# Mixture-of-experts kernel on one core: the first expert product contracts 128 + 64 channels instead of 96 + 96, the 64 in the two row halves of the array

## The chip, the core and the metric

The kernel runs on one core of a Trainium2 chip. Times are device microseconds (us) of a whole run of the program; lower is better. The engines of the core work side by side, each through its own list of instructions: TensorE (PE in the profile, its weight loads PEld), VectorE (DVE), ScalarE (ACT), GpSimd (POOL) and SyncE (SP, which here only issues DMAs).

## The reference

The input is 8 sequences of 3584 tokens with 192 channels, all float32. A causal convolution over 7 tokens with softmaxed weights, one set of taps for each of 8 heads of 24 channels, makes `x`. A router chooses one of 8 experts for each token, and the expert's two-layer network is applied to it:

```python
logits = np.einsum('bsd,de->bse', x, w_gate)
local_gate = 1.0 / (1.0 + np.exp(-np.einsum('bsd,de->bse', x, w_local).squeeze(-1)))
for b in range(B):
    prev_e = -1
    for s in range(S):
        fresh_e = int(np.argmax(logits[b, s]))
        e = fresh_e if s == 0 or local_gate[b, s] < 0.5 else prev_e
        prev_e = e
        p = softmax(logits[b, s])                  # sum has 1e-9 added
        h = np.maximum(x[b, s] @ w1[e], 0.0)       # w1[e]: 192 x 1024
        out[b, s] = p[e] * (h @ w2[e])             # w2[e]: 1024 x 192
```

A token with an open local gate takes the expert of the token before it.

## The kernel before

It has three stages, one after the other.

**Convolve and route** (`convolve_and_route`, lines 103 to 265). One sequence at a time, 28 tiles of 128 tokens. The convolution is a product with two banded 128 x 128 matrices a head (L165, L167), taken out of PSUM by ScalarE and VectorE alternately (L172, L170) into `y_sb`, a tile with one row of 193 values a token: 192 channels, then the gate. `y_sb` is transposed on TensorE (L177), moved to SBUF (L181, L183) and multiplied by the router's weights (L186, 9 columns). `route` works out each token's expert on VectorE, with four small transposes on TensorE (L222 to L242), writes the softmax value into the row's last column (L251) and stores the rows in DRAM as `rows` (L253, on ScalarE's DMA queue).

**Place** (`place`). Every token gets a slot; each expert's slots are filled up to whole blocks of 256. `slot_tok` holds the token of each slot, `blk_e` the expert of each block.

**Experts** (`experts`). 119 blocks of 256 slots, one after the other:

- `load` (two blocks ahead): SyncE's queue fetches the block's `w1b` (96 partitions x 2 x 1024) and `w2b`, three buffers of each; GpSimd gathers the block's 256 rows from DRAM in two indirect DMAs into `xg` (L393, four buffers).
- `hidden`: `hT = relu(w1.T x)`, 8 chunks of 128 of the 1024 hidden values. Each chunk is two matmuls of 96 contracted channels by 256 tokens (L414); two chunks share a PSUM tile `hps` of one bank, taken out in turn by ScalarE (L419) and VectorE (L417).
- `turn`: four transposes on TensorE (L402) turn the next block's `xg` into `xps`, and VectorE copies it to `xT` (L405).
- `output`: 16 matmuls of 128 hidden values by 192 channels (L426), the gate multiplied in by ScalarE (L434) and VectorE (L432), and two indirect DMAs by GpSimd that scatter the rows to `out` (L437).

The order on TensorE is the order of the code: `hidden` of block i, `turn` of block i + 1, `output` of block i. Each float32 matmul stands in the profile as two weight loads and two matmul records, so the 16 matmuls of `hidden` are 32 records a block; a transpose is one record.

Of the kernel before, what the change touches and what calls it, by code (L numbers as in the profile page):

```python
# [8 lines left out]
F32 = mybir.dt.float32  # L9
BF16 = mybir.dt.bfloat16  # L10
# [12 lines left out]
GS = D // H             # channels of a head  # L23
N = B * S               # tokens
NT = S // P             # tiles of 128 tokens in a sequence
T = N // P              # tiles of 128 tokens in all
DH = D // 2             # the contraction over D goes in two halves
FK = F // P
CB = NT // 2            # tiles that one convolution matmul takes
BT = 256                # slots of a block; all slots of a block go to one expert  # L30
KT = BT // P
NB = (N + E * (BT - 1)) // BT   # blocks that suffice however the tokens fall
NS = NB * KT            # tiles of 128 slots
DG = D + 1              # a token's row: its D values, then its gate
# [4 lines left out]
def bcast(ap, n):  # L39
    """[p, a] -> [p, a, n]"""  # L40
    return ap.rearrange("p (a o) -> p a o", o=1).to_broadcast([ap.shape[0], ap.shape[1], n])


def bcast_mid(ap, n):
    """[p, a] -> [p, n, a]"""
    return ap.rearrange("p (o a) -> p o a", o=1).to_broadcast([ap.shape[0], n, ap.shape[1]])


def conv_bands(nc, cst, scr, weight):
    """The causal convolution as two matrices a head: band takes a tile of tokens  # L50
    to itself, pband the tile before to it."""
    w = scr.tile([P, H, KC], F32, name="w")
    nc.sync.dma_start(out=w, in_=weight.partition_broadcast(P))
    wm = scr.tile([P, H], F32, name="wm")
    nc.vector.tensor_reduce(wm, w, axis=AX.X, op=Alu.max)
    nc.vector.tensor_tensor(w, w, bcast(wm, KC), op=Alu.subtract)
    nc.scalar.activation(w, w, Act.Exp)
    ws = scr.tile([P, H], F32, name="ws")
    nc.vector.tensor_reduce(ws, w, axis=AX.X, op=Alu.add)
    nc.vector.tensor_scalar(ws, ws, 1e-9, None, Alu.add)  # L60
    nc.vector.reciprocal(ws, ws)
    c = scr.tile([P, H, KC], F32, name="c")
    nc.vector.tensor_tensor(c, w, bcast(ws, KC), op=Alu.mult)

    band = cst.tile([P, H, P], F32, name="band")
    pband = cst.tile([P, H, P], F32, name="pband")
    for dst, j0, shift in ((band, 0, 0), (pband, 1, P)):
        for j in range(j0, KC):
            # 1 where column - row = j - shift
            m = scr.tile([P, P], F32, name="m", bufs=2)  # L70
            nc.gpsimd.memset(m, 0.0)
            nc.gpsimd.affine_select(out=m, in_=m, compare_op=Alu.not_equal, fill=1.0,
                                    base=shift - j, pattern=[[1, P]], channel_multiplier=-1)
            for h in range(H):
                tap = c[:, h, KC - 1 - j:KC - j]
                if j == j0:
                    nc.vector.tensor_scalar(dst[:, h, :], m, tap, None, Alu.mult)
                else:
                    nc.vector.scalar_tensor_tensor(dst[:, h, :], m, tap, dst[:, h, :],  # L79
                                                   Alu.mult, Alu.add)  # L80
    return band, pband


@with_exitstack
def kernel(
    ctx: ExitStack,
    tc: tile.TileContext,
    x: bass.AP,
    weight: bass.AP,
    wgl: bass.AP,  # L90
    w1: bass.AP,
    w2: bass.AP,
    out: bass.AP,
):
    nc = tc.nc
    keep = ctx.enter_context(tc.tile_pool(name="keep", bufs=1))
    dram = ctx.enter_context(tc.tile_pool(name="dram", bufs=1, space=DRAM))
    # every token's row by its number; row N is zero and stands for an empty slot
    rows = dram.tile([N + 1, DG], F32, name="rows")

    ident = keep.tile([P, P], F32, name="ident")
    make_identity(nc, ident)
    # 1 where token t * 128 + p goes to expert e
    oh_all = keep.tile([P, E, T], F32, name="oh_all")
    slot_tok = keep.tile([P, NS], I32, name="slot_tok")
    blk_e = keep.tile([1, NB], I32, name="blk_e")

    with ExitStack() as one:
        convolve_and_route(one, tc, x, weight, wgl, rows, ident, oh_all)
    with ExitStack() as two:  # L110
        place(two, tc, oh_all, slot_tok, blk_e)
    with ExitStack() as three:
        experts(three, tc, w1, w2, out, rows, ident, slot_tok, blk_e)


def convolve_and_route(ctx, tc, x, weight, wgl, rows, ident, oh_all):
# [27 lines left out]
    # 8 * (place in the sequence) + 9  # L144
# [5 lines left out]
    # e and 8 - e  # L150
# [7 lines left out]
    def conv(x_sb):  # L158
        y_sb = ys.tile([P, NT, DG], F32, name="y_sb")
        lps = lps_p.tile([P, NT, E + 1], F32, name="lps")  # L160
        for s in range(0, NT, CB):
            for h in range(H):
                hc = slice(h * GS, (h + 1) * GS)
                cps = cps_p.tile([P, CB, GS], F32, name="cps")
                nc.tensor.matmul(cps, lhsT=band[:, h, :], rhs=x_sb[:, 1 + s:1 + s + CB, hc],  # L165
                                 start=True, stop=False)
                nc.tensor.matmul(cps, lhsT=pband[:, h, :], rhs=x_sb[:, s:s + CB, hc],  # L167
                                 start=False, stop=True)
                if h % 2:
                    nc.vector.tensor_copy(y_sb[:, s:s + CB, hc], cps)  # L170
                else:
                    nc.scalar.copy(y_sb[:, s:s + CB, hc], cps)  # L172
        for j in range(0, NT, 2):
            tps = tps_p.tile([DH, 2, 2, P], F32, name="tps")
            for u in range(2):
                for k in range(2):
                    nc.tensor.transpose(tps[:, u, k, :], y_sb[:, j + u, k * DH:(k + 1) * DH],  # L177
# [12 lines left out]
    def route(b, y_sb, lps):  # L190
# [5 lines left out]
        # the first of the largest logits: 8 - max over them of (8 - e)  # L196
# [5 lines left out]
        # the gate is under 1/2 where its logit is under 0; a sequence's first token chooses  # L202
# [3 lines left out]
        # tokens that choose: 8 * place + expert; the others: -1  # L206
# [3 lines left out]
        # softmax's exponentials and the reciprocal of their sum  # L210
# [8 lines left out]
        # the largest key so far is that of the last token that chose: a tile of  # L219
        # tokens to a partition, and the tiles before by their largest keys  # L220
# [30 lines left out]
        nc.vector.tensor_tensor(y_sb[:, :, D], pr, rs, op=Alu.mult)  # L251
# [17 lines left out]
def place(ctx, tc, oh_all, slot_tok, blk_e):  # L269
    """A slot for every token: the experts' tokens one expert after the other, each  # L270
    expert's slots filled up to whole blocks. slot_tok[p, n] is the token in slot
    n * 128 + p, N where there is none; blk_e the blocks' experts."""
# [5 lines left out]
    # constants  # L278
    ones = wk.tile([P, P], F32, name="ones")
    nc.vector.memset(ones, 1.0)  # L280
    tri = wk.tile([P, P], F32, name="tri")      # 1 where row < column
# [6 lines left out]
    countb = wk.tile([P, NS], BF16, name="countb")      # whole numbers under 256  # L288
# [6 lines left out]
    # a token's rank among its expert's: those before in its partition, then all  # L295
    # of the partitions before
# [12 lines left out]
    # each expert's blocks and where they begin  # L309
# [11 lines left out]
    # cum counts the token itself and the experts before it too  # L321
# [16 lines left out]
    # a block's expert: how many of the first 7 end at or before it  # L338
# [7 lines left out]
    # token t * 128 + p into slot hi * 128 + lo: the sum over the tokens of  # L346
    # (1 at lo) x (t + 1 and p at hi). All are whole numbers up to 256, exact in
    # bf16, and one token at most meets a slot.
# [20 lines left out]
def experts(ctx, tc, w1, w2, out, rows, ident, slot_tok, blk_e):  # L369
# [9 lines left out]
    MH = 512 // BT  # L379

    def load(i):
        e = nc.values_load(blk_e[0:1, i:i + 1], engines=[ET.SP], min_val=0, max_val=E - 1,
                           skip_runtime_bounds_check_because="a count of at most 7")
        w1b = wp.tile([DH, 2, F], F32, name="w1b")
        nc.sync.dma_start(out=w1b.rearrange("p k f -> p (k f)"),
                          in_=w1[bass.ds(e, 1)].rearrange("o p x -> (o p) x"))
# [11 lines left out]
    def turn(i, xg):  # L398
        xps = xps_p.tile([DH, 2, BT], F32, name="xps")
        for d in range(2):  # L400
            for k in range(KT):
                nc.tensor.transpose(xps[:, d, k * P:(k + 1) * P],  # L402
                                    xg[:, k, d * DH:(d + 1) * DH], identity=ident)
        xT = tp.tile([DH, 2, BT], F32, name="xT")
# [3 lines left out]
    def hidden(w1b, xT):  # L408
        hT = hp.tile([P, FK, BT], F32, name="hT")
        for m in range(0, FK, MH):  # L410
            hps = hps_p.tile([P, MH, BT], F32, name="hps")
            for u in range(MH):
                for d in range(2):
                    nc.tensor.matmul(hps[:, u, :], lhsT=w1b[:, d, (m + u) * P:(m + u + 1) * P],  # L414
                                     rhs=xT[:, d, :], start=(d == 0), stop=(d == 1))
            if (m // MH) % 2:
                nc.vector.tensor_scalar(hT[:, m:m + MH, :], hps, 0.0, None, Alu.max)  # L417
            else:
                nc.scalar.activation(hT[:, m:m + MH, :], hps, Act.Relu)  # L419
        return hT  # L420

    def output(i, w2b, xg, hT):
# [6 lines left out]
        for k in range(KT):  # L429
            gate = xg[:, k, D:D + 1]  # L430
# [5 lines left out]
            # an empty slot's number, N, is out of bounds: nothing is written for it  # L436
# [16 lines left out]

# [25 lines left out]
```

## Time and profile before

| what | value |
|---|---|
| time, median of 3 runs (lowest, highest) | 2085.78 us (2084.18, 2089.68) |
| span of the profiled execution, first to last instruction | 2076.4 us |
| TensorE matmul busy, share of the span | 1953.5 us, 94% |
| VectorE, ScalarE, GpSimd busy | 594.2, 257.6, 494.7 us |
| mean granted TensorE clock over the span | 0.934 |
| moved by DMA | 278.60 MB, mean 134 GB/s |

The time of the profiled execution as the three runs measure it was not recorded; its span is 9.4 us under their median, which is what lies around the first and last instruction. A row of the profile's groups reads: line, engine, operation, output<-input tiles, shapes, count | busy us, mean ns of one | idle us of the engine just before them and who ended the idle time. "96\*128 96x256" of a matmul is the shape of the weights, then of the moving data. The records of successive matmuls overlap: a record goes on for a while after the next one has started, so the step from one start to the next is what a stream costs, not the mean of one record.

### The profile page before, as it was taken

How to read it: one execution, taken by the hardware profiler on the slowest of the kernel's cores; microseconds unless marked ns; L12 is line 12 of the kernel's file. 1: busy time of each engine (PE TensorE's matmuls, PEld its weight loads, DVE VectorE, ACT ScalarE, POOL GpSimd, SP SyncE). 2: the span in 40 equal slices, each digit the busy share in tenths (PEclk: the TensorE clock that was granted, in tenths of full speed). 3: DMA queues.
4: the chain of work that ended last, by engine and by line, in shares of the span. 5: the costliest groups of instructions: out<-in, count | busy, mean ns of one | idle time of the engine just before them, and what ended most of it. 6: DMA issues, size and time to landing. Idle time of an engine off the chain costs nothing. (4 is left out here: it accounts for less than half of the span.)

```text
span 2076.4 us, 25966 instructions
## 1 busy us (share of the span) xinstructions
PE 1953.5 (94%) x10208; PEld 1679.0 (81%) x10208; DVE 594.2 (29%) x1648; ACT 257.6 (12%) x487; POOL 494.7 (24%) x521
## 2 busy tenths in 40 slices
PE   2989889589699999999999999999999999999998
PEld 1868667511199999999999999999999999999997
DVE  5333333599711111111111112111111211111111
ACT  0211112000011111111111111111111111111111
POOL 3000000000123333333333333333333333333331
PEclk9989879555599999999999999999999999999999
DMA  3362441300265555555555555555555555555551
GB/s 107 104 160 88 130 121 40 98 9 1 61 175 152 160 162 156 154 159 157 153 155 163 157 153 156 163 155 153 162 161 154 153 160 158 152 158 163 156 154 34
DMA packets 111547, 278.60 MB, mean 134 GB/s; under 512 B 12639, under 2 KB 77367, under 8 KB 100002
## 3 DMA queue, kind: packets, MB, share of 16 engines
q1 hardware_dynamic: 59536, 209.24, 34.3%
q0 software_dynamic: 22848, 45.58, 7.5%
q10 hardware_dynamic: 29042, 22.14, 4.4%
q8 instruction: 80, 1.31, 0.3%
q14 instruction: 41, 0.34, 0.0%
HBM read 232.74 MB, written 45.53 MB: 134 GB/s over the span
## 5 line engine op out<-in xcount | busy, mean ns | idle before, releaser
L414 PE MATMUL hps<-xT,w1b 96*128 96x256 f32 x3808 | 843.2, 379 | 0.0
L414 PEld LDWEIGHTS hps<-xT,w1b 96*128 96x128 f32 x3808 | 721.2, 190 | 93.3
L426 PE MATMUL yps<-w2b,hT 128*128 128x192 f32 x3808 | 638.5, 326 | 0.0
L426 PEld LDWEIGHTS yps<-w2b,hT 128*128 128x128 f32 x3808 | 616.1, 190 | 0.1
L437 POOL DMA_INDIRECT out_dram<-o_sb,slot_tok x238 | 240.6, 1011 | 963.4 <-ACT o_sb L434 859.1
L417 DVE TENSOR_SCALAR hT<-hps 128x512 f32<-128x512 f32 x238 | 164.5, 691 | 638.3 <-PE hps L414 638.3
L393 POOL DMA_INDIRECT xg<-rows,slot_tok x238 | 232.9, 979 | 230.2 <-DVE slot_tok L366 154.5
L419 ACT ACTIVATE hT<-hps 128x512 f32<-128x512 f32 x238 | 142.1, 597 | 675.8 <-PE hps L414 673.0
L432 DVE TENSOR_SCALAR o_sb<-yps,xg 128x192 f32<-128x192 f32 x119 | 49.7, 418 | 572.7 <-ACT o_sb L434 572.7
L434 ACT ACTIVATE o_sb<-yps,xg 128x192 f32<-128x192 f32 x119 | 50.0, 420 | 804.9 <-PE yps L426 784.5
L358 PE MATMUL sps<-at_hi,at_lo 128*128 128x476 bf16 x224 | 124.4, 555 | 24.5 <-DVE at_lo L352 13.0
L186 PEld LDWEIGHTS lps<-wg,yT 96*128 96x128 f32 x896 | 126.7, 215 | 16.5 <-ACT yT L183 8.0
L165 PE MATMUL cps<-x_sb,band 128*128 128x336 f32 x256 | 100.8, 478 | 31.2 <-DVE band L79 27.1
L186 PE MATMUL lps<-wg,yT 96*128 96x9 f32 x896 | 123.3, 265 | 3.8 <-DVE yT L181 3.4
L358 PEld LDWEIGHTS <-at_lo 128*128 128x128 bf16 x224 | 23.4, 105 | 124.7 <-DVE at_lo L352 124.7
L167 PE MATMUL cps<-x_sb,pband 128*128 128x336 f32 x256 | 98.2, 467 | 10.2 <-DVE pband L79 10.2
L165 PEld LDWEIGHTS cps<-x_sb,band 128*128 128x128 f32 x256 | 48.4, 201 | 52.6 <-DVE band L79 27.3
L402 PE MATMUL xps<-ident,xg 128*96 128x128 f32 x476 | 73.3, 275 | 13.6 <-DMA xg<-rows,slot_tok 13.6
L405 DVE COPY xT<-xps 96x512 f32<-96x512 f32 x119 | 80.5, 676 | 13.4 <-PE xps L402 13.4
L402 PEld LDWEIGHTS xps<-ident,xg 128*96 128x96 f32 x476 | 56.6, 127 | 29.3 <-issue 11.8
L167 PEld LDWEIGHTS cps<-x_sb,pband 128*128 128x128 f32 x256 | 49.4, 200 | 33.0 <-DVE pband L79 11.4
L177 PE MATMUL tps<-ident,y_sb 128*96 128x128 f32 x448 | 75.4, 295 | 0.0
(114 smaller groups left out, 532.4 us busy)
## 6 DMA issues: line engine op xcount, KB each, us to landing
w1b<-in_w_dram SPq DMA_DIRECT2D x119, 768.0 KB, 5.2
w2b<-in_w_dram SPq DMA_DIRECT2D x119, 768.0 KB
rows<-y_sb ACTq DMA_DIRECT2D x16, 1351.0 KB, 7.7
x_sb<-in_x_dram SPq DMA_DIRECT2D x16, 1344.0 KB, 6.5
xg<-rows,slot_tok POOLq DMA_INDIRECT x238, 9.1
out_dram<-o_sb,slot_tok POOLq DMA_INDIRECT x238, 2.4
w<-in_weight_dram SPq DMA_DIRECT2D x1, 28.0 KB
wg<-in_wgl_dram ACTq DMA_DIRECT2D x1, 6.8 KB
```

The source lines that it names most:

```text
L165: nc.tensor.matmul(cps, lhsT=band[:, h, :], rhs=x_sb[:, 1 + s:1 + s + CB, hc], start=True, stop=False)
L167: nc.tensor.matmul(cps, lhsT=pband[:, h, :], rhs=x_sb[:, s:s + CB, hc], start=False, stop=True)
L186: nc.tensor.matmul(lps[:, j + u, :], lhsT=yT[:, u, k, :], rhs=wg[:, k, :], start=(k == 0), stop=(k == 1))
L358: nc.tensor.matmul(sps, lhsT=at_lo, rhs=at_hi, start=(t == 0), stop=(t == T - 1))
L393: nc.gpsimd.indirect_dma_start(out=xg[:, k, :], out_offset=None, in_=rows[:, :], in_offset=bass.IndirectOffsetOnAxis(ap=slot_tok[:, n:n + ...
L402: nc.tensor.transpose(xps[:, d, k * P:(k + 1) * P], xg[:, k, d * DH:(d + 1) * DH], identity=ident)
L405: nc.vector.tensor_copy(xT, xps)
L414: nc.tensor.matmul(hps[:, u, :], lhsT=w1b[:, d, (m + u) * P:(m + u + 1) * P], rhs=xT[:, d, :], start=(d == 0), stop=(d == 1))
L417: nc.vector.tensor_scalar(hT[:, m:m + MH, :], hps, 0.0, None, Alu.max)
L419: nc.scalar.activation(hT[:, m:m + MH, :], hps, Act.Relu)
L426: nc.tensor.matmul(yps[:, k, :], lhsT=hT[:, m, k * P:(k + 1) * P], rhs=w2b[:, m, :], start=(m == 0), stop=(m == FK - 1))
L437: nc.gpsimd.indirect_dma_start(out=out, out_offset=bass.IndirectOffsetOnAxis(ap=slot_tok[:, n:n + 1], axis=0), in_=o_sb[:, k, :], in_offse ...
```

## The change

The 192 channels are contracted as 128 + 64. The first 128 take one matmul a chunk over the whole height of the array. The other 64 take half its height, and two chunks of F are given to the two halves: rows 0 to 63 hold one chunk's weights, rows 64 to 127 another's. The moving data must then stand in both halves of the partitions, so a token's row in DRAM holds its last 64 channels twice (257 values: gate, 192 channels, 64 again), and `w1` is laid out on the host to match.

```diff
-DG = D + 1              # a token's row: its D values, then its gate
+DR = D - P
+DG = 1 + D + DR
 ... conv, for each half of a sequence: y_sb's channels start at column 1
+            nc.gpsimd.tensor_copy(y_sb[:, s:s + CB, 1 + D:], y_sb[:, s:s + CB, 1 + P:1 + D])
 ... load
-        w1b = wp.tile([DH, 2, F], F32, name="w1b")
+        w1b = wp.tile([P, F + F // 2], F32, name="w1b")
 ... turn
-        xps = xps_p.tile([DH, 2, BT], F32, name="xps")
+        xps = xps_p.tile([P, 2, BT], F32, name="xps")
-                                    xg[:, k, d * DH:(d + 1) * DH], identity=ident)
+                                    xg[:, k, 1 + d * P:1 + (d + 1) * P], identity=ident)
 ... hidden
-        for m in range(0, FK, MH):
-            hps = hps_p.tile([P, MH, BT], F32, name="hps")
-            for u in range(MH):
-                for d in range(2):
-                    nc.tensor.matmul(hps[:, u, :], lhsT=w1b[:, d, (m + u) * P:(m + u + 1) * P],
-                                     rhs=xT[:, d, :], start=(d == 0), stop=(d == 1))
-            if (m // MH) % 2:
-                nc.vector.tensor_scalar(hT[:, m:m + MH, :], hps, 0.0, None, Alu.max)
-            else:
-                nc.scalar.activation(hT[:, m:m + MH, :], hps, Act.Relu)
+        hps = [hps_p.tile([P, 2, BT], F32, name="hps") for q in range(FK // 2)]
+        for s in range(FK):
+            nc.tensor.matmul(hps[s // 2][:, s % 2, :], lhsT=w1b[:, s * P:(s + 1) * P],
+                             rhs=xT[:, 0, :], start=(s % 2 == 0), stop=False,
+                             skip_group_check=True)
+        for half in range(2):
+            for j in range(2):
+                for row in range(2):
+                    rows_ = slice(row * DR, (row + 1) * DR)
+                    c = F + (half * 2 + j) * P
+                    nc.tensor.matmul(hps[half * 2 + row][:, j, :], lhsT=w1b[rows_, c:c + P],
+                                     rhs=xT[rows_, 1, :], start=False, stop=True,
+                                     skip_group_check=True)
+            for row in range(2):
+                q = half * 2 + row
+                if row:
+                    nc.vector.tensor_scalar(hT[:, 2 * q:2 * q + 2, :], hps[q], 0.0, None, Alu.max)
+                else:
+                    nc.scalar.activation(hT[:, 2 * q:2 * q + 2, :], hps[q], Act.Relu)
```

The gate is read from column 0 instead of column 192, and the router's transposes start at column 1. `_w1_layout` puts rows 0 to 127 of an expert's `w1` into the first 1024 columns, and into the other 512 the remaining 64 rows of the chunk pairs, one chunk of a pair on the upper 64 partitions and one on the lower; the bytes of an expert's weights stay the same.

TensorE's list in the expert stage, one block before the change: the four `hps` tiles of `hidden` (16 matmuls), the transposes, `output`. The numbers in the names count the tiles.

```order
L414 MATMUL hps_7061<-xT_7022,w1b_6917 128x256 x4
L414 MATMUL hps_7067<-xT_7022,w1b_6917 128x256 x4
L414 MATMUL hps_7073<-xT_7022,w1b_6917 128x256 x4
L414 MATMUL hps_7079<-xT_7022,w1b_6917 128x256 x4
L402 MATMUL xps_7085<-ident_61,xg_6989 96x128 x4
L426 MATMUL yps_7092<-w2b_6919,hT_7060 128x192 x16
```

The same place after the change (L415 is the matmul over 128 channels, L424 the one over 64):

```order
L415 MATMUL hps_5853<-xT_5814,w1b_5709 128x256 x2
L415 MATMUL hps_5854<-xT_5814,w1b_5709 128x256 x2
L415 MATMUL hps_5855<-xT_5814,w1b_5709 128x256 x2
L415 MATMUL hps_5856<-xT_5814,w1b_5709 128x256 x2
L424 MATMUL hps_5853<-xT_5814,w1b_5709 128x256
L424 MATMUL hps_5854<-xT_5814,w1b_5709 128x256
L424 MATMUL hps_5853<-xT_5814,w1b_5709 128x256
L424 MATMUL hps_5854<-xT_5814,w1b_5709 128x256
L424 MATMUL hps_5855<-xT_5814,w1b_5709 128x256
L424 MATMUL hps_5856<-xT_5814,w1b_5709 128x256
L424 MATMUL hps_5855<-xT_5814,w1b_5709 128x256
L424 MATMUL hps_5856<-xT_5814,w1b_5709 128x256
```

There are still 16 matmuls of 256 columns, but the last eight alternate between the array's upper and lower half, each half with its own PSUM tile, and the first `hps` tile is complete after 11 of them instead of after 4.

GpSimd's list in the first stage, before (the last masks of the convolution's bands, then the zeroed first tiles of the following sequences' `x_sb`):

```order
L72 AFFINE_SELECT m<-m 128x128
L129 MEMSET x_sb 128x192 x6
L285 IOTA ii 128x238
```

and after:

```order
L73 AFFINE_SELECT m<-m 128x128
L175 COPY y_sb<-y_sb 128x14x64
L130 MEMSET x_sb 128x192
L175 COPY y_sb<-y_sb 128x14x64 x2
L130 MEMSET x_sb 128x192
L175 COPY y_sb<-y_sb 128x14x64 x2
```

Sixteen copies of 14 x 64 values a partition stand between the memsets now; the list of VectorE and that of ScalarE hold the same instructions as before.

More of the change, by code (lines that the diff above doesn't have):

```diff
@@ L163, in conv @@
                 hc = slice(h * GS, (h + 1) * GS)
+                yc = slice(1 + h * GS, 1 + (h + 1) * GS)
                 cps = cps_p.tile([P, CB, GS], F32, name="cps")
@@ L169, in conv @@
                 if h % 2:
-                    nc.vector.tensor_copy(y_sb[:, s:s + CB, hc], cps)
+                    nc.vector.tensor_copy(y_sb[:, s:s + CB, yc], cps)
                 else:
-                    nc.scalar.copy(y_sb[:, s:s + CB, hc], cps)
+                    nc.scalar.copy(y_sb[:, s:s + CB, yc], cps)
+            nc.gpsimd.tensor_copy(y_sb[:, s:s + CB, 1 + D:], y_sb[:, s:s + CB, 1 + P:1 + D])
         for j in range(0, NT, 2):
@@ L176, in conv @@
                 for k in range(2):
-                    nc.tensor.transpose(tps[:, u, k, :], y_sb[:, j + u, k * DH:(k + 1) * DH],
+                    nc.tensor.transpose(tps[:, u, k, :], y_sb[:, j + u, 1 + k * DH:1 + (k + 1) * DH],
                                         identity=ident)
@@ L250, in route @@
         nc.vector.tensor_reduce(pr, ex, axis=AX.X, op=Alu.add)
-        nc.vector.tensor_tensor(y_sb[:, :, D], pr, rs, op=Alu.mult)
+        nc.vector.tensor_tensor(y_sb[:, :, 0], pr, rs, op=Alu.mult)
         for s in range(0, NT, CB):
@@ L378, in experts @@
     yps_p = ctx.enter_context(tc.tile_pool(name="yps_p", bufs=2, space=PSUM))
-    MH = 512 // BT
     def load(i):
@@ L383, in load @@
                            skip_runtime_bounds_check_because="a count of at most 7")
-        w1b = wp.tile([DH, 2, F], F32, name="w1b")
-        nc.sync.dma_start(out=w1b.rearrange("p k f -> p (k f)"),
-                          in_=w1[bass.ds(e, 1)].rearrange("o p x -> (o p) x"))
+        w1b = wp.tile([P, F + F // 2], F32, name="w1b")
+        nc.sync.dma_start(out=w1b, in_=w1[bass.ds(e, 1)].rearrange("o p x -> (o p) x"))
         w2b = wp.tile([P, FK, D], F32, name="w2b")
@@ L402, in turn @@
                 nc.tensor.transpose(xps[:, d, k * P:(k + 1) * P],
-                                    xg[:, k, d * DH:(d + 1) * DH], identity=ident)
-        xT = tp.tile([DH, 2, BT], F32, name="xT")
+                                    xg[:, k, 1 + d * P:1 + (d + 1) * P], identity=ident)
+        xT = tp.tile([P, 2, BT], F32, name="xT")
         nc.vector.tensor_copy(xT, xps)
@@ L429, in output @@
         for k in range(KT):
-            gate = xg[:, k, D:D + 1]
+            gate = xg[:, k, 0:1]
             if k % 2:
@@ L451, in experts, with _w1_layout @@
         output(i, w2b, xg, hT)
+def _w1_layout(np, w1):
+    rest = w1[:, P:, :].reshape(E, DR, 2, 2, 2, P)
+    rest = rest.transpose(0, 3, 1, 2, 4, 5).reshape(E, P, F // 2)
+    return np.concatenate([w1[:, :P, :], rest], 2)
 def kernel(**inputs):
@@ L466 @@
         .reshape(2, DH, E + 1).transpose(1, 0, 2).reshape(DH, 2 * (E + 1)),
-        "w1": i["moe_w1"].reshape(E, 2, DH, F).transpose(0, 2, 1, 3).reshape(E, DH, 2 * F),
+        "w1": _w1_layout(_np, i["moe_w1"]),
         "w2": i["moe_w2"].reshape(E, FK, P, D).transpose(0, 2, 1, 3).reshape(E, P, FK * D),
```

## The prediction

> **What bounds the kernel now.** I read the page's busy times and groups first, then busy times by stage, then the order of time inside one expert block.
>
> ```profile
> span 2076.4 us, 25966 instructions
> PE 1953.5 (94%) x10208; PEld 1679.0 (81%) x10208; DVE 594.2 (29%) x1648; ACT 257.6 (12%) x487; POOL 494.7 (24%) x521
> PEclk9989879555599999999999999999999999999999
> L414 PE MATMUL hps<-xT,w1b 96*128 96x256 f32 x3808 | 843.2, 379 | 0.0
> L414 PEld LDWEIGHTS hps<-xT,w1b 96*128 96x128 f32 x3808 | 721.2, 190 | 93.3
> L426 PE MATMUL yps<-w2b,hT 128*128 128x192 f32 x3808 | 638.5, 326 | 0.0
> L402 PE MATMUL xps<-ident,xg 128*96 128x128 f32 x476 | 73.3, 275 | 13.6 <-DMA xg<-rows,slot_tok 13.6
> ```
>
> The two expert products have no idle time before them: 0.0 in the last column. The first one (L414), which the change rewrites, covers 843.2 us, 41% of the span.
>
> ```profile
> 39.00:410.00 371.00, 329.39 (x1888) 265.81 (x1888) 135.58 (x378) 63.94 (x128) 5.48 (x9) 0.86 0.37 100
> 566.00:2052.00 1486.00, 1482.36 (x8014) 1375.03 (x8015) 282.82 (x472) 190.07 (x353) 463.76 (x466) 1.00 0.54 156
> ```
>
> These are busy times by stage (length, then PE, PEld, DVE, ACT, POOL, then granted clock, DMA share, GB/s). In the expert stage TensorE is busy 1482 of 1486 us at the full clock, while DMA stands at 0.54 and no other engine passes a third. What a block costs TensorE is what the stage costs. One block in order of time:
>
> ```profile
> 1201.02 7.07 PE L414 MATMUL hps<-xT,w1b 96*128 96x256 f32 x32
> 1206.40 0.60 ACT L419 ACTIVATE hT<-hps 128x512 f32<-128x512 f32 x1 [2.81 <-PE hps L414]
> 1207.92 0.60 PE L402 MATMUL xps<-ident,xg 128*96 128x128 f32 x4
> 1208.12 0.69 DVE L417 TENSOR_SCALAR hT<-hps 128x512 f32<-128x512 f32 x1 [2.76 <-PE hps L414]
> 1208.36 5.37 PE L426 MATMUL yps<-w2b,hT 128*128 128x192 f32 x32
> 1208.73 0.68 DVE L405 COPY xT<-xps 96x512 f32<-96x512 f32 x1
> 1213.57 2.75 PE L414 MATMUL hps<-xT,w1b 96*128 96x256 f32 x12
> ```
>
> The block's period is 1213.57 - 1201.02 = 12.55 us. The 32 records of L414 take 7.07 us, the last of them 0.379 to its end: 31 steps in 6.69 us, 0.216 us a step. A step is the time of 256 columns whether 96 rows or 128 are filled, which L426 bears out: it has 128 rows and 192 columns, and 31 steps in 5.37 - 0.33 us make 0.163 us, 192/256 of 0.216. So contracting 128 instead of 96 costs nothing, and only the count of steps matters.
>
> **The change part by part.**
>
> *First eight matmuls (128 channels).* 16 records at 0.216 us: 3.46 us, half of the old 6.91.
>
> *Last eight (64 channels).* Again 16 records; before they were 16 x 0.216 = 3.46 us. No row of this trace has two matmuls in two halves of the array, so the cost is bounded. From above: one after the other, 3.46 us. From below: full overlap in pairs. The two records of one matmul use the same rows, so they follow each other; the second record of one matmul can run with the first record of the next, which is in the other half. With starts in program order that makes 16 records into a chain of 9 steps, 9 x 0.216 = 1.94 us. There are still 16 weight loads, though, and loads have a rate of their own:
>
> ```profile
> 249.32 0.97 PEld L186 LDWEIGHTS lps<-wg,yT 96*128 96x128 f32 x8
> 249.43 0.96 PE L186 MATMUL lps<-wg,yT 96*128 96x9 f32 x8
> 251.31 1.03 PEld L186 LDWEIGHTS lps<-wg,yT 96*128 96x128 f32 x8 [0.20 <-ACT yT L183]
> 251.49 0.96 PE L186 MATMUL lps<-wg,yT 96*128 96x9 f32 x8
> ```
>
> These matmuls stream 9 columns, so loads set the pace: eight in 0.97 us, the last 0.19 long, 0.112 us a load. Two loads for each step of two matmuls are 0.224 us, a little over the step's 0.216. I take 8 x 0.224 + 0.216 = 2.01 us, near the low bound, because nothing but that load rate lies between. The stage saves 3.46 - 2.01 = 1.45 us a block.
>
> *Going to half height and back.* Each block goes from whole-height matmuls to half-height ones, and back for the transposes. The nearest rows are those of the router, where a transpose on 28 rows stands between matmuls on 128:
>
> ```profile
> 97.93 0.95 PE L177 MATMUL tps<-ident,y_sb 128*96 128x128 f32 x7
> 98.81 0.07 PEld L227 LDWEIGHTS rps<-ident,last 28*1 28x1 f32 x1 [0.18 <-issue]
> 98.92 0.19 PEld L167 LDWEIGHTS cps<-x_sb,pband 128*128 128x128 f32 x1
> 98.92 0.55 PE L167 MATMUL cps<-x_sb,pband 128*128 128x336 f32 x1
> 81.92 0.45 PE L167 MATMUL cps<-x_sb,pband 128*128 128x336 f32 x1
> ```
>
> Seven transposes in 0.95 us, the last 0.27 long, step 0.11; the last starts at 98.61, and a follower would start at 98.72. The load for L227 starts only at 98.81, having waited for nothing that the profile shows ("issue"): 0.09 us late, and a load that normally lies under the matmul before it is exposed. The exposed load shows on the way back: that L167 record is 0.55 long instead of 0.45, 0.10 more. So one change of height costs 0.09 + 0.10, about 0.20 us with 128 columns of weights, and a block has two: 0.40 us. Bounds: nothing from below; from above the whole tail of a matmul (0.379 - 0.216 = 0.16) and a load in full, from its start to its matmul's, 251.49 - 251.31 = 0.18: 0.34 each. I take 0.20, since the rows are the same event.
>
> The Trainium skill, "TensorEngine Tiling (Array Packing)", Key Properties, says that changing the tiling mode drains the engine, while going from tile to tile in one mode does not. That speaks against the change, and the late loads above agree with it; the page has no figure. If a drain meant the whole tail and load, the sum would be 0.28 us a block, 33 us in all, worse than with my price.
>
> *Transposes.* 128 columns of weights instead of 96, so they go at the load's 0.112 us rather than 0.109: 0.01 us a block. The copy to `xT` has 512 elements a partition as before.
>
> *Evictions.* ScalarE's first and VectorE's first now start late, at the end of the first half of the paired matmuls, about 1 us before `hidden` ends, and the second of each at its end. ScalarE's take 0.60 us, VectorE's 0.69. `output` starts after the transposes, some 0.5 us later, and needs its first two tiles then, its third after four more matmuls (4 x 2 x 0.163 = 1.3 us): both are there. VectorE's copy to `xT` stands behind its second eviction as before (1208.12, then 1208.73), with 5 us of `output` as cover. The `hps` tiles are free again long before the next `hidden`. Cost nothing; without that cover it would be the 0.69 us of one eviction.
>
> *DMAs and GpSimd.* Weights: same bytes. Rows are 257 values instead of 193, a third more.
>
> ```profile
> rows<-y_sb ACTq DMA_DIRECT2D x16, 1351.0 KB, 7.7
> ACT y_sb L172 <- DMA rows<-y_sb: 15.5, 3, 6.8
> PE cps L165 <- ACT y_sb L172: 2.8, 2, 2.5
> xg<-rows,slot_tok POOLq DMA_INDIRECT x238, 9.1
> PE xps L402 <- DMA xg<-rows,slot_tok: 13.6, 4, 10.6
> L72 POOL TENSOR_SCALAR_AFFINE_SELECT m<-m 128x128 f32<-128x128 f32 x13 | 12.0, 924 | 0.8
> L129 POOL MEMSET x_sb<- 128x192 f32 x8 | 2.1, 257 | 231.6 <-PE cps L167 231.6
> ```
>
> A row store takes 7.7 us to land; a third more is 2.6. ScalarE waited three times for one, and through it TensorE 2.8 us: 0 to 8 us more, I take 3. A gather takes 9.1 us and is issued a block or more ahead of a stage with DMA at 0.54; only the first one is waited for (10.6), 0 to 3 us more, I take 1. GpSimd's 16 copies have 896 elements: by the memset's rate (257 ns for 192) 1.2 us each, by the mask's (924 for 128) 6.5 us, 19 to 104 us in a stage where GpSimd works 5.5 of 371 us. Who waits for a copy is the row store, which comes after the next sequence's convolution; behind it on GpSimd stands a memset needed a sequence later. I count nothing; if copies held up the last stores, 5 us.
>
> *Sum.* A block: -1.45 + 0.40 + 0.01 = -1.04 us; 119 blocks: -124 us; stages one and three's start: +4. That is -120 us: span 2076.4 to 1956, and with the 9.4 us between span and median, 2085.8 to 1966 us. Its own bounds: no price for the change of height and loads not limiting, (3.46 - 1.94) x 119 = 180 less, 1905; 0.34 each way and +11 outside, (1.45 - 0.69) x 119 - 11 = 79 less, 2007.
>
> **The rivals.**
>
> *The halves do not overlap.* Each half-height record takes its 0.216 us in turn, and the change adds two changes of height for nothing: (0.40 + 0.01) x 119 + 4 = +53, 2139 us, slower (bounds +5 to +88). It decides as soon as the 16 records take over 3.46 - 0.41 = 3.05 us, 0.19 a record. For it: no overlap stands in this trace, and each float32 matmul is two records in the same rows. Against it: loads already run under matmuls here, so parts of the array are fed independently. The Trainium skill, "TensorE: Matmul & The Clock Gate", Part 3, measured 3.07 times for four row tiles of 32, starting about 4 ns apart, matmuls starting and ending in program order. No run here shows that yet; by it the chain of 9 steps stands.
>
> *The halves overlap, but a load is not brought forward past a waiting matmul.* Then the other half's load starts only when the second record before it does, and its matmul follows 0.112 to 0.18 us behind: each matmul costs 0.216 + 0.112 to 0.18, eight 2.62 to 3.17 us. By the middle, 2.90, a block gains 0.56 - 0.41 = 0.15 us; by the fast end 0.43; by the slow end it loses 0.12. The fast end is nearer, since loads in a stream went at 0.112: some 0.33 x 119 - 4 = 35 us less, 2050 us (2039 to 2104). For it: in L414's stream a load's time ends within its step (721.2 us of loads in 843.2 us of matmuls). Against it: in the L186 rows the loads run a whole step ahead of the matmuls (249.32 and 249.43, with steps of 0.11).
>
> *Something else takes the place of TensorE.* At 11.5 us a block DMA's share would go from 0.54 to about 0.61 with the longer rows, GpSimd's from 463.76/1486 to 0.34. Neither bounds; under 2 in 100.
>
> **How the numbers follow.** Sum: 0.62. No overlap: 0.18. Loads not brought forward: 0.18. Rest: 0.02. The prediction is the sum's, 1966 us; its own range 1905 to 2007. To leave out no more than 2 in 10, the range also takes in most of the third case: 1895 to 2078. Under 0.3%, 6 us, this kernel's runs, which spread over 5.5 us, can't tell a change from none. Faster: the sum's 0.62, most of the third case (0.16) and half the rest: 0.79. Same: 0.03. Slower: 0.18.
>
> **What would show it.** In the changed profile the block's period should be 11.5 us, L415's step 0.216, L424's 16 records about 2.0 us, with pairs of records starting close together; before the first L424 load and before the first transpose a gap of about 0.1 us on PEld with "issue". L424 at 3.4 us a block would show the first rival; 2.6 us or more, with each load 0.1 us before its matmul, the second. I would be wrong too if `output` began to wait for `hT`, or if the first stage (now 39 to 410) grew by more than 10 us.

## The result, and the profile after

The changed kernel takes 1925.3 us (median of 4 runs, 1921.3 to 1925.48), the kernel before 2084.98 us beside it (4 runs): a ratio of 0.9239, 95% interval 0.9217 to 0.9262. It is 160 us faster; the forecast was 120 us, 1966 us. The page of the changed kernel, its span, engines and costliest lines on TensorE:

```profile
span 1923.8 us, 26008 instructions
PE 1795.3 (93%) x10208; PEld 1488.1 (77%) x10208; DVE 595.0 (31%) x1648; ACT 257.8 (13%) x487; POOL 510.1 (27%) x537
L439 PE MATMUL yps<-w2b,hT 128*128 128x192 f32 x3808 | 638.8, 326 | 0.0
L415 PE MATMUL hps<-xT,w1b 128*128 128x256 f32 x1904 | 432.6, 380 | 0.0
L424 PE MATMUL hps<-xT,w1b 64*128 64x256 f32 x1904 | 237.7, 389 | 0.0
L424 PEld LDWEIGHTS hps<-xT,w1b 64*128 64x128 f32 x1904 | 174.1, 186 | 55.3 <-issue 39.5
```

The 843.2 us of the old first product have become 432.6 + 237.7 = 670.3 us. L415 costs about what half of the old matmuls cost (421.6), although it fills 128 rows instead of 96. L424 has as many records as L415 and covers little more than half the time: its records run two at a time. In the block below, the first two start at 1214.065 and 1214.072, the next two at 1214.385 and 1214.392. So do its loads: 1904 of 186 ns would be 354 us one after the other, and they cover 174.1; the first two start at 1214.064 and 1214.070.

One block of the changed kernel in order of time:

```profile
1210.52 3.62 PE L415 MATMUL hps<-xT,w1b 128*128 128x256 f32 x16
1214.06 1.60 PEld L424 LDWEIGHTS hps<-xT,w1b 64*128 64x128 f32 x16 [0.33 <-issue]
1214.07 2.00 PE L424 MATMUL hps<-xT,w1b 64*128 64x256 f32 x16
1215.27 0.69 DVE L430 TENSOR_SCALAR hT<-hps 128x512 f32<-128x512 f32 x1 [3.68 <-PE hps L424]
1215.28 0.60 ACT L432 ACTIVATE hT<-hps 128x512 f32<-128x512 f32 x1 [4.14 <-PE hps L424]
1215.99 0.42 PEld L404 LDWEIGHTS xps<-ident,xg 128*128 128x128 f32 x4 [0.33 <-DMA xg<-rows,slot_tok]
1215.99 0.66 PE L404 MATMUL xps<-ident,xg 128*128 128x128 f32 x4
1216.49 5.37 PE L439 MATMUL yps<-w2b,hT 128*128 128x192 f32 x32
1221.69 2.54 PE L415 MATMUL hps<-xT,w1b 128*128 128x256 f32 x11
```

The period is 1221.69 - 1210.52 = 11.17 us instead of 12.55. L424's 16 records take 2.00 us from the first start to the last end. Take off one record's tail and an exposed load (0.38 + 0.10) and 1.52 us is left, seven steps of 0.217: eight pairs, one every 0.216 us. So the matmuls of L424 cost 8 x 0.216 = 1.73 us of TensorE's time; the 2.00 us of the row also hold the tail and the exposed load. The changes of height can be read too. L415's last record started at 1213.76 (3.62 less 0.38 after 1210.52), a follower would have started at 1213.98, and the load for L424 starts at 1214.06, 0.08 to 0.09 us late, put down to "issue"; that load is exposed for 0.10. On the way back the transposes' load starts 0.08 us after the step would have ended (1216.07 - 0.38 + 0.22 = 1215.91), and the four take 0.66 us instead of 0.60. Together about 0.34 us a block. "DMA xg" stands there as the releaser, but the same gap is put down to "issue" on the way in, and in the experiments below it stays 0.33 long whatever is named.

Outside the blocks: the first stage's row stores, what ScalarE waits for, GpSimd's copies, and when the place stage's matmuls start (row stores and start of before: 7.7 us, and 420.1).

```profile
rows<-y_sb ACTq DMA_DIRECT2D x16, 1799.0 KB, 11.3
ACT y_sb L174 <- DMA rows<-y_sb: 22.6, 3, 7.8
PE cps L167 <- ACT y_sb L174: 9.8, 3, 3.6
L175 POOL COPY y_sb<-y_sb 128x896 f32<-128x896 f32 x16 | 15.0, 940 | 275.9 <-DVE y_sb L172 275.9
L361 PE MATMUL sps<-at_hi,at_lo x224: 554/557/580, 433.8 to 569.2; 128*128 128x476 bf16 x112
```

In this execution the first stage ends some 14 us later than in the profile of before, with TensorE's wait for ScalarE, and through it for a row store, grown from 2.8 to 9.8 us. The copies cost GpSimd 0.94 us each, and nobody waits for them.

### The profile page after: what moved, and what is told of

Same layout as the page of the kernel before. It is cut to its first block, busy times and chain, and to the rows that moved or that the text cites. A ratio compares the mean times of both kernels' runs of the same rounds, so it can differ in the third digit from the quotient of the medians.

```text
span 1923.8 us, 26008 instructions
## 1 busy us (share of the span) xinstructions
PE 1795.3 (93%) x10208; PEld 1488.1 (77%) x10208; DVE 595.0 (31%) x1648; ACT 257.8 (13%) x487; POOL 510.1 (27%) x537
## 5 line engine op out<-in xcount | busy, mean ns | idle before, releaser
L439 PE MATMUL yps<-w2b,hT 128*128 128x192 f32 x3808 | 638.8, 326 | 0.0
L439 PEld LDWEIGHTS yps<-w2b,hT 128*128 128x128 f32 x3808 | 616.0, 190 | 0.7 <-ACT hT L432 0.7
L415 PE MATMUL hps<-xT,w1b 128*128 128x256 f32 x1904 | 432.6, 380 | 0.0
L415 PEld LDWEIGHTS hps<-xT,w1b 128*128 128x128 f32 x1904 | 360.2, 191 | 43.7
L424 PE MATMUL hps<-xT,w1b 64*128 64x256 f32 x1904 | 237.7, 389 | 0.0
L424 PEld LDWEIGHTS hps<-xT,w1b 64*128 64x128 f32 x1904 | 174.1, 186 | 55.3 <-issue 39.5
L404 PEld LDWEIGHTS xps<-ident,xg 128*128 128x128 f32 x476 | 50.6, 142 | 51.4 <-DMA xg<-rows,slot_tok 38.0
L359 DVE TENSOR_SCALAR at_hi<-countb,hi,pf 128x238 bf16<-128x238 bf16 x224 | 90.1, 402 | 0.0
L404 PE MATMUL xps<-ident,xg 128*128 128x128 f32 x476 | 79.6, 289 | 10.7 <-DMA xg<-rows,slot_tok 10.7
```

Of the source, the lines that this page charges most:

```text
L404: nc.tensor.transpose(xps[:, d, k * P:(k + 1) * P], xg[:, k, 1 + d * P:1 + (d + 1) * P], identity=ident)
L415: nc.tensor.matmul(hps[s // 2][:, s % 2, :], lhsT=w1b[:, s * P:(s + 1) * P], rhs=xT[:, 0, :], start=(s % 2 == 0), stop=False, skip_group_c ...
L424: nc.tensor.matmul(hps[half * 2 + row][:, j, :], lhsT=w1b[rows_, c:c + P], rhs=xT[rows_, 1, :], start=False, stop=True, skip_group_check=True)
L439: nc.tensor.matmul(yps[:, k, :], lhsT=hT[:, m, k * P:(k + 1) * P], rhs=w2b[:, m, :], start=(m == 0), stop=(m == FK - 1))
```

## The experiments

**Is it the overlap?** The eight 64-channel matmuls all in the upper half of the array:

```diff
-                    rows_ = slice(row * DR, (row + 1) * DR)
+                    rows_ = slice(0, DR)
```

> The eight 64-channel matmuls all use array rows 0 to 63 (the odd chunks so multiply the wrong weights and the output is not the reference's); nothing else differs from the changed kernel. Theory, the gain is the overlap of the two halves: without it L424 goes from 8 steps of 0.216 us to 16, +1.73 us a block, 119 blocks: +206 us, 2131 us, slower than the kernel before by about 46 us (two changes of height, 0.35 us a block). Rival, a half-height matmul is simply quicker by itself: L424 stays near 2.0 us a block and the time near 1925 us.

Measured: 2123.8 us, ratio 1.0196 to the kernel before (1.0175 to 1.0216). Its L424 in the page's groups, and in one block:

```profile
L424 PE MATMUL hps<-xT,w1b 64*128 64x256 f32 x1904 | 442.4, 382 | 0.0
1203.56 3.32 PEld L424 LDWEIGHTS hps<-xT,w1b 64*128 64x128 f32 x16 [0.33 <-issue]
1203.57 3.72 PE L424 MATMUL hps<-xT,w1b 64*128 64x256 f32 x16
```

Sixteen steps, 3.72 us instead of 2.00. A half-height matmul alone is as long as a whole one (382 ns a record, 0.216 us a step). The time is 202 us over the changed kernel's 1921.7 us (timed again further down), 1.70 us a block where eight steps more are 1.73. Without the overlap the change costs 2%, which is the first rival's case.

**Does the order within the pairs matter?** Two matmuls of one half, then two of the other:

```diff
-            for j in range(2):
-                for row in range(2):
+            for row in range(2):
+                for j in range(2):
```

> The same eight matmuls in another order: two of one half, then two of the other, instead of alternating. Theory A, each half of the array has its own queue and takes its records whenever they are there: 8 steps as now, 1925 us. Theory B, matmuls start in the order of the program, and only neighbours in different halves overlap: 13 steps of 0.216 us, +1.08 us a block, 2053 us.

Measured: 1930.3 us, ratio 0.9274 (0.9259 to 0.9290). One block of it:

```profile
1211.26 1.70 PEld L424 LDWEIGHTS hps<-xT,w1b 64*128 64x128 f32 x16 [0.33 <-issue]
1211.27 2.10 PE L424 MATMUL hps<-xT,w1b 64*128 64x256 f32 x16
1213.30 0.66 PE L404 MATMUL xps<-ident,xg 128*128 128x128 f32 x4
```

2.10 us, half a step more than 2.00 and nothing like the 3.1 of starts in the list's order (13 steps, the tail and the exposed load). TensorE's list as built has the matmuls in the order of this edit. The second matmul of one half doesn't hold up the first of the other half behind it. In this block the first eight records start in four pairs 0.01 us apart, as if both halves had begun at once. Then one record, at 1212.25, lasts 0.47 us like the first of a stretch instead of 0.38, and its load starts only 0.01 us before it: the 0.10 us is one more exposed load. The records don't say which half they belong to, so that the halves take their work independently is read from these times alone.

**What does a change of height cost?** Four whole, four half, four whole, four half:

```diff
-        for s in range(FK):
-            nc.tensor.matmul(...)          # all eight over 128 channels first
         for half in range(2):
+            for s in range(half * 4, half * 4 + 4):
+                nc.tensor.matmul(...)
```

> Four full-height matmuls, four half-height, four full, four half: four changes of height a block instead of two, same matmuls. Theory, each change costs 0.15 to 0.20 us on TensorE (late load and exposed load): +0.35 to 0.39 us a block, +41 to +46 us, 1966 to 1971 us. Rival, the gap before L424 and the transposes is a wait for something else (a semaphore, the gather): the new changes cost nothing, 1925 us.

Measured: 1968.8 us, ratio 0.9453 (0.9437 to 0.9469), 43.5 us over the changed kernel's first 1925.3 us and 47 over the 1921.7 us of its second timing: 0.37 to 0.40 us a block for two changes more. One block, first its loads, each change with the same gap, then its first matmuls and its transposes:

```profile
1207.62 0.73 PEld L423 LDWEIGHTS hps<-xT,w1b 64*128 64x128 f32 x8 [0.33 <-issue]
1208.68 1.59 PEld L416 LDWEIGHTS hps<-xT,w1b 128*128 128x128 f32 x8 [0.33 <-issue]
1210.61 0.73 PEld L423 LDWEIGHTS hps<-xT,w1b 64*128 64x128 f32 x8 [0.33 <-issue]
1211.67 0.42 PEld L404 LDWEIGHTS xps<-ident,xg 128*128 128x128 f32 x4 [0.33 <-issue]
1205.80 1.89 PE L416 MATMUL hps<-xT,w1b 128*128 128x256 f32 x8
1211.67 0.65 PE L404 MATMUL xps<-ident,xg 128*128 128x128 f32 x4
```

From the first matmul to the transposes it takes 1211.67 - 1205.80 = 5.87 us, against 1215.99 - 1210.52 = 5.47 in the changed kernel: 0.40 us for the two changes, the prediction's 0.20 each. One of the two goes back to whole-height matmuls with 256 columns, not to transposes.

**What do the longer rows cost alone?** The kernel before with the new row (gate first, 64 channels twice, 257 values) and its own 96 + 96 matmuls; the diff is the change's without `load`, `turn`'s shapes and `hidden`.

> The kernel before with only the longer rows: gate in column 0, the 64 channels twice, GpSimd's 16 copies, 257 values stored and gathered; matmuls as before (96 + 96). Theory from the changed trace: stage one ends some 11 to 14 us later, the blocks stay at 12.55 us: 2096 to 2099 us. Rival, the price in the prediction: +4 us, 2089 us; nothing if stage one's end moved by chance.

Measured: 2088.0 us against 2082.9, ratio 1.0030 (1.0017 to 1.0043): 5 us, as the prediction priced it, and not the 14 of one profile. The place stage's first matmul starts at 425.5 us here. In seven profiles of kernels with long rows it starts at 425 to 434 us, in the five with short rows at 420 to 428: the first stage's end varies by several us from run to run, and the long rows add about 6 to it on average. Much of the rest goes with TensorE's clock: by the trace the granted clock falls to a half three times between 110 and 325 us, for 61.5 us in all in the profile of before and for 75.1 in that of after. At half the clock 13.6 us more cost about 7, by estimate, which with the rows comes near the 14. Over all the profiles the drops are 58 to 75 us with long rows and 62 to 72 with short ones, so the rows are not shown to lengthen them. The wait is the same as above:

```profile
PE cps L167 <- ACT y_sb L174: 10.1, 3, 4.2
```

**Can the rows stay short? A first try.** Rows of 193 values, and VectorE doubles the 64 channels inside `xg`, ahead of `hidden`. In part:

```diff
+    def twice(xg):
+        nc.vector.tensor_copy(xg[:, :, DG:], xg[:, :, 1 + P:DG])
 ...
+        if i + 1 < NB:
+            twice(got[i + 1][2])
         hT = hidden(w1b, xT)
```

> The changed kernel with rows of 193 values again (gate first): nothing is copied, stored or gathered twice; instead VectorE copies the 64 channels inside xg, one instruction of 128 x 2 x 64 a block, a block ahead of the transposes. Theory, what the longer rows cost is the rows' stores in stage one: about 5 us come back (the first stage as in the kernel before), the copy of some 0.3 us a block hides on VectorE, 1920 us. Rival, the copy gets in the way of an eviction that TensorE waits for: 0.3 us a block, 1955 us.

Measured: 2028.4 us, ratio 0.9742 (0.9730 to 0.9755), 107 us slower than the changed kernel timed beside it (1921.7). One block, and what VectorE waited for in all:

```profile
1204.22 0.98 POOL L393 DMA_INDIRECT xg<-rows,slot_tok  x1 [0.31 <-issue]
1204.26 2.00 PE L426 MATMUL hps<-xT,w1b 64*128 64x256 f32 x16
1207.00 0.23 DVE L399 COPY xg<-xg 128x128 f32<-128x128 f32 x1 [5.21 <-DMA xg<-rows,slot_tok]
1207.14 1.28 DVE L432 TENSOR_SCALAR hT<-hps 128x512 f32<-128x512 f32 x2
1207.88 4.82 PE L441 MATMUL yps<-w2b,hT 128*128 128x192 f32 x28 [0.38 <-DVE hT L432]
DVE xg L399 <- DMA xg<-rows,slot_tok: 644.7, 119, 9.8
```

My expectation missed by far. In VectorE's list as built the copy of the block three ahead stands before this block's evictions, although the code has it two blocks later: the scheduler had moved it up to its gather. VectorE therefore waits 5.21 us for a gather that GpSimd has just issued; its two evictions, the first due at about 1205.5, come after 1207.1, and `output` waits. The copy itself takes 0.23 us. The rival named the right victim and a price (0.3 us a block) three times too small. The block shown is 0.65 us longer than in the changed kernel. The mean of 0.9 holds a few longer waits too: in this stage the granted clock fell to a half four times, for 6.8 us each, at blocks in which TensorE waited 3.1 to 5.0 us for an eviction (after a wait of 4.50 us, `output`'s 28 records took 7.86 us instead of 4.82), while the changed kernel's stayed full from 588 us to the end of the stage.

**One stretch at half height for two blocks.** 128 channels of block i, 64 of block i, 64 of block i + 1, and the 128 of block i + 1 later on top; six `hps` banks, one `xps`, one `yps`. Weights and gathers are also fetched four blocks ahead instead of two, with more buffers. In outline:

```diff
+        full(w1a, xT[i], hpsa, hTa, False)            # start of the sum
+        halves(w1a, xT[i], hpsa, hTa, True)           # end of it, evictions
+        halves(w1b, xT[i + 1], hpsb, None, False)     # start of the next block's
+        ready(i + 2); output(i, ...)
+        full(w1b, xT[i + 1], hpsb, hTb, True)         # end of it, evictions
+        ready(i + 3); output(i + 1, ...)
```

> Blocks in pairs: 128 channels of block i, 64 of block i, 64 of block i+1, then 128 of block i+1 later, on top of its 64. One stretch at half height serves two blocks, so two changes of height for two blocks instead of four; six hps banks, one xps, one yps. Theory, a change costs 0.15 to 0.20 us of TensorE each: 0.17 us a block less, 20 us, 1905 us. Rival, with one bank each for xps and yps TensorE waits for evictions (about 0.7 us each, once a block): 1925 us or more.

Measured: 1901.5 us, ratio 0.9129 (0.9117 to 0.9141), 20 us under the changed kernel's 1921.7. One stretch of it:

```profile
1201.89 3.32 PEld L433 LDWEIGHTS hps<-xT,w1b 64*128 64x128 f32 x32 [0.33 <-issue]
1201.89 3.72 PE L433 MATMUL hps<-xT,w1b 64*128 64x256 f32 x32
1205.55 0.66 PE L404 MATMUL xps<-ident,xg 128*128 128x128 f32 x4
1223.88 0.30 PEld L433 LDWEIGHTS hps<-xT,w1b 64*128 64x128 f32 x4 [0.33 <-issue]
```

Thirty-two records in 16 steps (3.72 us, what 16 records took in the same half), with one gap for two blocks. Two blocks take 1223.88 - 1201.89 = 21.99 us instead of 2 x 11.17 = 22.34, and 59 pairs make 21 us of that. The deeper fetching was not tried alone. But the two changes of height that are gone cost 0.34 us in the changed kernel, and TensorE was already busy there without a break (200.00 of 200 us in each stretch from 600 to 1800 us), so it had little to give.

**Pairs and the copy inside `xg`.**

> Both of these edits together. Theory, they are independent: 20 us and 5 us less than the changed kernel, 1900 us. Rival, VectorE's copy delays a copy of xps, of which there is only one now: 1910 to 1940 us.

Measured: 2017.1 us, ratio 0.9684 (0.9657 to 0.9711). The copy brings its wait along (VectorE waits 589 us for gathers in all), 116 us over the pairs alone; neither guess held.

**The changed kernel again, beside these.**

> The changed kernel itself, timed beside the three above. Theory: 1925 us, 0.924 of the kernel before; the start of the place stage lies anywhere from 5 to 14 us later than in the kernel before's profile. Rival, the first profile's 14 us are the true price of the longer rows: again 434 us.

Measured: 1921.7 us, ratio 0.9231 (0.9219 to 0.9243), its place stage starting its matmuls at 427.3 us.

**Short rows without a wait.** Rows of 193 values again. The second pair of transposes takes channels 64 to 191, so the last 64 land in partitions 64 to 127, and the copies out of PSUM place them twice. In part:

```diff
-                                    xg[:, k, 1 + d * P:1 + (d + 1) * P], identity=ident)
+                                    xg[:, k, 1 + d * DR:1 + d * DR + P], identity=ident)
-        nc.vector.tensor_copy(xT, xps)
+        nc.vector.tensor_copy(xT[:, 0, :], xps[:, 0, :])
+        nc.scalar.copy(xT[:DR, 1, :], xps[P - DR:, 1, :])
+        nc.vector.tensor_copy(xT[DR:, 1, :], xps[P - DR:, 1, :])
```

> The changed kernel with rows of 193 values and no copy of xg: the second pair of transposes takes channels 64 to 191, so the last 64 land in partitions 64 to 127, and the copy to xT becomes three, after the transposes (VectorE 128 x 256, ScalarE 64 x 256 shifted to partitions 0 to 63, VectorE 64 x 256). Theory, the copy inside xg lost its time only because VectorE stood waiting for a gather with the evictions behind it; nothing waits here, so what is left is what the longer rows cost, about 5 us: 1917 us. Rival, the extra ScalarE and VectorE instructions delay TensorE as before: 1950 us or more.

Measured: 1915.1 us, ratio 0.9195 (0.9182 to 0.9207), 6.6 us under the changed kernel's 1921.7; the two were not timed side by side, but the intervals of their ratios lie apart (one ends at 0.9207, the other begins at 0.9219). The blocks' period is as it was, 11.17 us: the three copies, 0.43, 0.41 and 0.37 us, hide under `output`. The place stage's first matmul starts at 421.4.

```profile
L408 DVE COPY xT<-xps 64x256 f32<-64x256 f32 x119 | 50.9, 428 | 58.2 <-ACT xT L407 58.2
L406 DVE COPY xT<-xps 128x256 f32<-128x256 f32 x119 | 49.3, 414 | 10.2 <-PE xps L403 10.0
L407 ACT COPY xT<-xps 64x256 f32<-64x256 f32 x119 | 43.8, 368 | 243.3 <-issue 181.4 <-DVE xT L406 60.2 <-DVE hT L431 1.7
```

**Both.**

> The pairs of blocks with the same short rows and shifted copies. Theory, the two gains add: 1901 less 5, 1896 us. Rival, with one bank for xps the three copies hold the next transposes up: 1901 us or more.

Measured: 1892.6 us, ratio 0.9093 (0.9081 to 0.9106), the fastest here: 29 us under the changed kernel's 1921.7, 189 under the kernel before.

## Why the prediction was right, and where its sizes were off

- *A step does not depend on the rows filled.* Held: L415 at 128 rows has the old step, (3.62 - 0.38) / 15 = 0.216 us.
- *The paired matmuls, 2.01 us.* Right mechanism, wrong size: 8 steps of 0.216, 1.73 us. Two terms failed. The chain of 9 steps took starts to be in the order of the list, first record, second record, next matmul; the pairs start together from the first record on, and the reordered matmuls above lose only half a step. The ninth step is 0.22 us. And the 0.224 us for two loads took the whole-height rate of 0.112 us a load to hold across the halves; loads of two halves go side by side (354 us of records in 174.1). That is the other 0.06. Together 0.28 us a block, 33 of the 40 us by which the forecast fell short. The 2.00 us of L424's row is near the sign the prediction gave, "about 2.0 us", by coincidence: the row covers the tail and the exposed load besides.
- *The range.* Its low end, 1905 us, took 1.94 us for the least that the pairs can cost, and they cost less. The time still lies inside because that end put the change of height at nothing, and it cost 0.34 us; that is luck.
- *The change of height, 0.20 us each.* Held on the way in (0.09 late, 0.10 exposed), a little less on the way back to transposes (0.15): 0.34 instead of 0.40 us a block, 7 us. Two changes more cost 0.40 us a block, 0.20 each, and one stretch for two blocks gave 20 us back, both as the price says.
- *Sum.* 3.46 - 1.73 - 0.34 = 1.39 us a block against a measured 12.55 - 11.17 = 1.38; 119 blocks 164 us, less about 5 for the rows: 159, measured 160.
- *Outside the blocks, 4 us.* The experiment that isolates the rows says 5 (0.17 to 0.43% of 2083, 4 to 9 us). The profile alone would have said 14 for the first stage, which the prediction named as a sign of being wrong; it is some 5 to 6 us for the rows and for the rest that stage's spread.
- *Evictions and GpSimd's copies at nothing.* Held: `output` follows the transposes without a wait (L439, 0.0 idle). A copy takes 0.94 us, less than the lower of my bounds.
- *The rivals.* "No overlap" is out for two halves: it is what 64 rows cost when one half does all the work, 2124 us (I had 2139; of its bounds +5 to +88, the upper is 86 by its own terms, 0.69 x 119 + 4). "Loads not brought forward" is out: after the first pair, L424's records follow in steps of 0.216 us, so no other load is exposed.
- *Readings that did not matter.* The 9.4 us between the span and the median of before is not what lies around the first and last instruction: in the runs timed later a time is 1.7 to 3.1 us over its span, so the profiled execution of before was a quick one. The forecast of 1966 us is 120 us off the median either way. And the row on the gathers shows four waits, 13.6 us in all, the longest 10.6, not one.

The Trainium skill's "TensorEngine Tiling (Array Packing)", Key Properties, says that tiles execute loads and matmuls in parallel, which the sum did not use and the trace bears out, and that changing the mode drains the engine, with which the load's 0.08 to 0.09 us of lateness here agrees. The Trainium skill's "TensorE: Matmul & The Clock Gate", Part 3, has matmuls starting strictly in program order; the reordered pairs, 2.10 us where that order gives 3.1, disagree, as far as the built list is the order in which TensorE gets them.

## What to carry to other kernels

On a kernel bound by TensorE, count steps of columns, not rows: with 64, 96 and 128 rows a step of 256 columns was 0.216 us here. A contraction of 192 as 128 + 64 paired costs 1.5 streams instead of 2, provided that the 64s of two outputs sit in opposite halves (here they also had PSUM tiles of their own; sharing one was not tried). Price each change of height at a late and an exposed load, 0.15 to 0.20 us here, and put the half-height work of several blocks together. An engine that is a third busy can still hold everything up by one instruction that waits for a DMA, as VectorE did with a copy of 0.23 us: look at where it stands in the engine's list, and at what stands behind it.

## What was not expected of the hardware

Weight loads into the two halves of the array overlap almost wholly: 16 loads of 187 ns in 1.60 us, the two of a pair starting 6 to 7 ns apart. (The 3.32 us of 16 loads into one half is the pace of the matmuls there, not of the loads.) And the halves need not be fed alternately: two matmuls in a row for one half, then two for the other, cost 0.10 us a block more.
